# Masked queries copied inside SBUF, transfers planned as one line of work, last set divided through a shuffle

## The chip, the cores and the metric

One core of a Trainium2 chip runs the whole kernel. The metric is the time of one execution on the device in microseconds (us); the median of the runs counts. The engines are PE (matrix multiply), ACT (activation functions), DVE (vector), POOL (GpSimd) and SP, which here only issues transfers.

## What is computed

```python
xn = _layernorm(A_x)                      # x: 1 x 2048 x 512, bf16
q, k, v = split(xn @ wqkv)                # 32 heads of 16
p = softmax(q @ k.T * 16 ** -0.5)         # per head, 2048 x 2048
A = (p @ v) @ wo
y = _layernorm(xn)
B = gelu(y @ w1 + b1) @ w2 + b2           # w1: 512 x 1792
out = A_x + A + B
```

There are 32 x 2048 x 2048 scores, 134 million, and each needs an exponential.

## The kernel before

**Tiling.** The queries come in four tiles of 512 columns. A *set* `g` is four heads of one query tile, so there are 32 sets, and a *unit* is one head of a set against 128 keys: a matmul of 32 rows (16 of a head, 16 of its neighbour) that gives 128x512 scores in one PSUM bank (`qk`, line 1163). There are 2048 units. A stored query tile holds two heads in 32 rows; for each of them a *masked* copy is needed in which the rows of the other one are zero, and this is `qz`.

**Two ways to an exponential.** Most units go to ACT, two or three banks in one instruction (line 1383). The rest go in fours to DVE, which approximates the exponential with integer arithmetic: one pass per unit (line 1480) and three passes over all four (line 1501), so that PE has four terms to add up where ACT leaves one (`pv`, line 1181). Which unit goes which way is settled while the program is built.

**The plan.** All instructions are put into the order of each engine by a planner, `_Plan`, that simulates the engines with durations written into the calls of `add`. `lat` is the time from the end of an instruction to its effect, above all from a transfer's issue to its landing. The table `PICK` overrides single choices: at step n it names the operation to take. Engines run strictly in the order so made, and so does the queue of SP: a transfer whose wait isn't over holds back all behind it.

**Masked queries** (`build_q`, lines 1018 to 1043). DVE scales the projected queries into `qc` (line 1031). A transfer writes `qc` into `zdram`, in DRAM, between rows that two transfers have set to zero at the start; two more read it back into `qz` at two row offsets, and so get the zeros along. They wait for the first to land. This happens 15 times.

**The other transfers on SP.** `ydram<-ys` writes the normalized rows for the MLP, 16 times; `ys` has two buffers, so DVE's next row (line 896) waits for the write of the last but one. For each pair of sets `build_opost` sends the sums to DRAM (`ldram`, line 1536), moves half the heads between partitions (`osb<-osb`, four transfers of 16x512, line 1540), reads the sums back in another shape (`lc`, line 1550), takes reciprocals (line 1554) and spreads them (`rdram`, `rlb`). The weights `w_r`, the bias and the outputs also go through SP.

**The last set** (`build_opost_last`) does without DRAM. In two halves of 256 columns DVE transposes 32x32 blocks out of PSUM (line 1598), takes the reciprocal of 8 columns of sums (1603), multiplies (1604) and transposes back (1607). POOL checks the sums (1613, 1615), and the result of all checks becomes a flag that decides whether a slow general version must run.

Of the kernel before, what the change touches and what calls it, by code (L numbers as in the profile page):

```python
# [50 lines left out]
class _Op:  # L51
# [3 lines left out]
                 "at", "feeds")  # L55
# [5 lines left out]
class _Plan:  # L61
# [28 lines left out]
    def add(self, eng, dur, fn, deps=(), prio=0.0, acq=(), rel=(), lat=0.0, dense=0.0, nb=0.0,  # L90
            mode=None, spare=False, feeds=False, hold=0):
        op = _Op()
        op.spare, op.feeds = spare, feeds
# [40 lines left out]
    def run(self):  # L134
# [8 lines left out]
        while self.left:  # L143
# [56 lines left out]
            op.end, op.at = end, t  # L200
            free[op.eng] = end
# [16 lines left out]

    pe_log = ()
# [266 lines left out]
def kernel(  # L486
# [47 lines left out]
    zdram = drp.tile([2, 2 * P, QW], BF, name="zdram")  # L534
# [88 lines left out]
    def act(cols):  # L623
# [1027 lines left out]
    def build_mlp(qt):  # L1651
# [44 lines left out]
        for x, (fc, n, pr) in enumerate(last):  # L1696
# [17 lines left out]
            if f1 > f0:  # L1714
                g = add("ACT", act((f1 - f0) * QW), lambda f0=f0, f1=f1: soft(1, f0, f1), [g], hi + 5)
# [203 lines left out]
```

## Time and profile before

| | us |
|---|---|
| median of 3 runs | 763.32 |
| lowest and highest run | 760.44, 763.65 |
| profiled execution | 769.47 |
| its span | 767.6 |
| PE busy in it | 736.1 (96%) |
| ACT busy | 736.0 (96%) |
| DVE busy | 701.0 (91%) |
| POOL busy | 47.4 (6%) |
| mean granted clock of PE | 0.989 |

The span runs from the first to the last instruction of the profiled execution; 1.9 us of its time lie outside. A part of what PE does is filler (lines 1318, 1857 and 1862, multiplications by zero), which the planner puts where PE would stand idle. So the busy share of PE says little, and the busy shares of ACT and DVE have to be read stretch by stretch.

### The profile page before, as it was taken

To read this page: it belongs to the slowest core of one execution; us is meant where nothing else is said; L and a number is where in the kernel's file an instruction comes from. 1 tells how busy PE (TensorE), PEld (TensorE's weight loads), DVE (VectorE), ACT (ScalarE), POOL (GpSimd) and SP (SyncE) were. 2 spreads that over 40 slices of the span, in tenths; PEclk is the share of its full clock that TensorE was granted. 3 is DMA by queue.
4 is the path that set the end of the run, shared out by engine and by line. 5 is a ranking of instruction groups with operands and counts; after the bars stand their busy time and mean duration, and the time that the engine had idled before them with its cause. 6 is when DMAs were issued, how large, how long until landed. Compare 5 with 4: busy or idle time off the path is not lost.

```text
span 767.6 us, 23191 instructions
## 1 busy us (share of the span) xinstructions
PE 736.1 (96%) x9941; PEld 246.1 (32%) x9943; DVE 701.0 (91%) x1187; ACT 736.0 (96%) x663; POOL 47.4 (6%) x78
## 2 busy tenths in 40 slices
PE   8999999999999999999998999999999999999997
PEld 4433333333332332233332233333322233333332
DVE  7968999999999998999888999989999999898895
ACT  6996999999999999999998999999999999999996
POOL 3500000000010010000002000000001000100010
PEclk9998999999999999999998999999999999999999
DMA  7233312102122341101055010102125202221001
GB/s 217 68 84 118 73 24 59 43 20 50 36 65 44 81 102 32 49 9 38 16 112 140 22 50 19 32 29 60 48 58 123 46 26 56 57 59 37 25 3 44
DMA packets 72858, 43.58 MB, mean 57 GB/s; under 512 B 49140, under 2 KB 65524, under 8 KB 72752
## 3 DMA queue, kind: packets, MB, share of 16 engines
q1 hardware_dynamic: 69456, 37.35, 18.4%
q0 software_dynamic: 2336, 4.20, 2.7%
q8 instruction: 78, 1.28, 0.7%
q10 hardware_dynamic: 960, 0.52, 0.3%
q14 instruction: 28, 0.23, 0.1%
HBM read 28.18 MB, written 7.19 MB: 46 GB/s over the span
## 4 chain that ended last, share of the span: by engine, by line
ACT 35%; PE 34%; DVE 13%; issue 12%; DMA 3%; SPq 1%; POOL 0%; DVEq 0%; ACTq 0%; POOLq 0%
ACT p_sb L1383 31%; PE ps L1181 12%; PE ps L1163 11%; PE ps L607 10%; DVE x_sb L1480 5%; DVE it L1501 4%; ACT ht L1688 2%; DMA lc<-ldram 1%; DVE it L1480 1%; ACT ht L1707 1%; DMA ydram<-ys 1%; PE ps L1862 1%; SPq L1540 1%; DMA ldram<-osb 1%; DVE osb L1534 1%
## 5 line engine op out<-in xcount | busy, mean ns | idle before, releaser
L1383 ACT ACTIVATE p_sb<-ps 128x1536 bf16<-128x1536 f32 (+1 forms) x619 | 695.8, 1272 | 16.6 <-PE ps L1163 15.1
L1163 PE MATMUL ps<-qz,kt 32*128 32x512 bf16 x2048 | 310.6, 385 | 18.7 <-ACT p_sb L1383 10.2
L1480 DVE TENSOR_SCALAR x_sb<-ps 128x512 int16<-128x512 f32 x420 | 279.0, 686 | 18.2 <-PE ps L1163 17.1
L1501 DVE TENSOR_SCALAR it<-x_sb 128x2048 int16<-128x2048 int16 x315 | 211.6, 690 | 3.1 <-PE ps L1181 2.0
L1163 PEld LDWEIGHTS <-kt 32*128 32x128 bf16 x2048 | 83.8, 91 | 271.5 <-issue 265.1
L1181 PE MATMUL ps<-p_sb,va 128*32 128x512 bf16 x1520 | 149.6, 392 | 0.8 <-DVE va L1063 0.4
L1181 PE MATMUL ps<-it,va 128*32 128x512 f16 x1692 | 137.7, 383 | 0.7 <-DVE it L1501 0.5
L1181 PEld LDWEIGHTS <-va 128*32 128x32 bf16 x3632 | 75.8, 95 | 135.7 <-issue 109.8
L1318 PE MATMUL ps<-ones_bf,zeros_bf 32*128 32x512 bf16 x280 | 101.5, 386 | 0.0
L1480 DVE TENSOR_SCALAR it<-ps 128x512 int16<-128x512 f32 x108 | 72.3, 686 | 5.2 <-PE ps L1163 4.8
L607 PE MATMUL ps<-yT,w_r 128*32 128x512 bf16 x896 | 59.2, 386 | 2.3 <-DVE x_sb L1480 1.8
L607 PE MATMUL ps<-w_sb,ht 128*32 128x512 bf16 x896 | 59.5, 381 | 0.0
L1501 DVE TENSOR_SCALAR it<-it 128x2048 int16<-128x2048 int16 x81 | 54.7, 688 | 0.8 <-PE ps L1181 0.4
L1729 POOL DMA_DIRECT2D wkv<-in_A_x_dram x16 | 16.7, 1056 | 448.1 <-DMA wkv<-b_f 325.3
L1181 PE MATMUL ps<-x_sb,va 128*32 128x512 f16 x420 | 41.9, 386 | 0.0
L1676 DVE TENSOR_SCALAR ht<-ps,b_sb 128x512 bf16<-128x512 f32 x40 | 29.9, 746 | 1.8 <-PE ps L607 1.7
L607 PEld LDWEIGHTS <-w_r 128*32 128x32 bf16 x896 | 21.0, 96 | 28.7 <-issue 14.3
L1862 PE MATMUL ps<-ones_bf,zeros_bf 128*32 128x512 bf16 x312 | 28.3, 386 | 0.0
L1318 PEld LDWEIGHTS <-zeros_bf 32*128 32x128 bf16 x280 | 24.7, 91 | 10.5 <-issue 9.8
L607 PEld LDWEIGHTS <-ht 128*32 128x32 bf16 x896 | 20.3, 96 | 23.5 <-issue 9.8
L1534 DVE COPY osb<-ps 128x512 f32<-128x512 f32 x31 | 21.3, 686 | 2.4 <-PE ps L1181 1.8
L607 PE MATMUL ps<-wkv,xnT 128*32 128x128 bf16 x1024 | 18.0, 225 | 0.9 <-DVE va L1063 0.8
(97 smaller groups left out, 296.6 us busy)
## 6 DMA issues: line engine op xcount, KB each, us to landing
w_r<-in_B_w_dram SPq DMA_DIRECT2D x56, 128.0 KB
rlb<-rdram SPq DMA_DIRECT2D x16, 256.0 KB
wkv<-b_f SPq DMA_DIRECT2D x16, 256.0 KB
wkv<-in_A_x_dram POOLq DMA_DIRECT2D x16, 256.0 KB, 3.9
qz<-zdram SPq DMA_DIRECT2D x30, 128.0 KB
ydram<-ys SPq DMA_DIRECT2D x16, 128.0 KB
zdram<-qc SPq DMA_DIRECT2D x15, 128.0 KB
osb<-osb SPq DMA_DIRECT2D x60, 32.0 KB
```

What stands on the lines that cost most here:

```text
L607: I(nc.tensor.matmul(dst[32 * j:32 * j + 32], lhsT=lhsT[:, 32 * j:32 * j + 32], rhs=rhs, start=start, stop=stop, tile_position=(0, 32 * j)))
L1163: I(nc.tensor.matmul(ps[:, bank, :], lhsT=kt[lo:lo + 32, s // 2, k * P:(k + 1) * P], rhs=qz[lo:lo + 32, (qt * NB + s // 2) % NQB, s % 2, : ...
L1181: I(nc.tensor.matmul(ps[32 * j:32 * j + 32, o_bank[g], :], lhsT=vals[:, h * VS:h * VS + 32], rhs=wts(j), start=pv_done[g] == 1, stop=end, ...
L1318: I(nc.tensor.matmul(ps[:, o_bank[g], :], lhsT=zeros_bf[32 * j:32 * j + 32, :], rhs=ones_bf[32 * j:32 * j + 32, :], start=False, stop=Fals ...
L1383: exp_inst.append(I(nc.scalar.activation(p_sb[:, s0:s1, :].rearrange("p a b -> p (a b)"), ps[:, b0:b0 + n, :].rearrange("p a b -> p (a b)" ...
L1480: I(nc.vector.tensor_scalar(out=ib[sl][:, j, :], in0=ps[:, pool.bank(key), :], scalar1=LEVEL, scalar2=0.0, op0=ALU.add, op1=ALU.max))
L1501: I(nc.vector.tensor_scalar(out=tb[x].rearrange("p j q -> p (j q)"), in0=ib[sl].rearrange("p j q -> p (j q)"), scalar1=float(SHIFT[t]), sc ...
L1534: e0 = add("DVE", dve(QW), lambda: I(nc.vector.tensor_copy(osb[:, e, :], ps[:, o_bank[g], :])), pv_ops[g] + list(osb_use.get(e, ())), pr - ...
L1676: I(nc.vector.tensor_scalar(out=hq[:, fc, :], in0=ps[:, misc.bank(key), :], scalar1=b1_sb[:, fc:fc + 1], scalar2=None, op0=ALU.add))
L1688: I(nc.scalar.activation(out=hv, in_=hv, func=AF.Gelu_apprx_tanh, scale=1.0))
L1729: return add("POOL", 1.0, lambda: I(nc.gpsimd.dma_start(out=acc[:, c, :], in_=x2[qi * P:(qi + 1) * P, :], accum_op=ALU.add)), (xb_,), pr - ...
L1862: I(nc.tensor.matmul(ps[32 * j:32 * j + 32, bank, :], lhsT=zeros_bf[:, 0:32], rhs=ones_bf[:], start=new, stop=new, tile_position=(0, 32 * ...
```

## The change

**Masked queries.** `zdram` and its transfers are gone. POOL sets three of the four `qz` buffers to zero once, and each time eight transfers of 16x512 copy the rows of a head from `qc` straight into `qz`, inside SBUF. Only these rows are ever written, so the zeros stay.

**Transfers in the planner.** Most transfers no longer have a fixed `lat`. They have `work`, the time that they occupy the DMA rings, and the planner lets them queue: one starts 0.5 us after its issue or when those ahead are through, and has landed 0.65 us after its work. ACT's gelu is planned 0.09 us longer.

**The last set.** For each half a shuffle copies the row of sums to the 32 rows of its group, DVE takes the reciprocal of all 256 columns and multiplies straight out of PSUM. The check is done behind both halves by DVE: one transpose of all 512 columns and two comparisons.

**Smaller things.** The accumulating transfers of `x` are planned one behind the other, POOL has a `drain` behind the last, and the identity matmuls at the end no longer wait in the plan for the last exponential but for the last scores. `PICK` is a new table, so the order is new on all engines; the constants that say which sets are meant for DVE are the same. The exponentials on ACT become 280 of three units and 336 of two.

```diff
+            if op.work is not None:
+                self.rings = max(end + self.DMA0, self.rings) + op.work
+                op.lat = self.rings + self.DMA1 - end
...
+    DMA0, DMA1 = 0.5, 0.65
+    rings = 0.0
...
-    zdram = drp.tile([2, 2 * P, QW], BF, name="zdram")
...
     PICK = {
-        29: 30, 69: 45, 83: 62, 86: 63, 99: 54, 104: 57, 107: 49, 128: 75, 130: 72, 133: 69, 141: 73,
+        64: 334, 65: 43, 127: 75, 158: 80, 169: 192, 170: 81, 173: 79, 185: 113, 191: 90, 197: 88,
...
             yw_op[t] = dma("SP", ydram[t * P:(t + 1) * P, :], ys[:, t % 2, :], (y_op[t],), prio=pr,
-                           lat=2.5)
+                           work=0.3)
...
+    mk_z = [None] + [add("POOL", 0.95, lambda n=n: I(nc.gpsimd.memset(qz[:, n], 0.0)), (), 10.0 + n, nb=12.0)
+                     for n in range(1, NQB)]
...
-        zd = zdram[n % 2]
-        w = dma("SP", zd.rearrange("(b z r) q -> b z r q", z=2, r=DH)[:, 0],
-                qc[:, n % 2, :], [e, mk_z[n % 2]] + qz_rd.get(n - 2, []), prio=pr - 600, lat=2.4)
...
         for par in range(2):
-            src = bass.AP(zd.tensor, zd.offset + par * DH * QW, [[4 * DH * QW, HS], [QW, 2 * DH], [1, QW]])
-            o = dma("SP", qz[:, n % NQB, par, :], src, [w] + old, prio=pr - 599 + par, lat=4.6)
+            for j in range(HS):
+                rows = slice(32 * j + DH * par, 32 * j + DH * par + DH)
+                o = dma("SP", qz[rows, n % NQB, par, :], qc[rows, n % 2, :],
+                        [e, mk_z[n] if n < NQB else None] + old, prio=pr - 600 + par, work=0.1)
+                qc_use[n].append(o)
...
         l_op[e] = add("SP", 0.5, lambda: I(nc.sync.dma_start(dram, osb[DH:P:32, e, :])), [e0], pr - 500,
-                      lat=L1)
+                      work=0.05)
...
-                 [l_op[0], l_op[e]], pr - 500, lat=L2)
+                 [l_op[0], l_op[e]], pr - 500, work=0.1)
...
-            e0 = add("DVE", 0.36, lambda qs=qs: I(nc.vector.transpose(
-                out=ta[:, qs], in_=ps[:, o_bank[g], qs])), pv_ops[g] + h_use[0] + [e1], pr,
-                rel=(o_done(g),) if hf else ())
...
+            def f0(qs=qs):
+                I(nc.vector.stream_shuffle(ta[:, qs], ps[:, o_bank[g], qs], [DH] * 32))
+            e0 = add("DVE", 0.4, f0, pv_ops[g] + h_use[0] + [e1], pr)
+
+            def f1(qs=qs):
+                I(nc.vector.reciprocal(out=ta[:, qs], in_=ta[:, qs]))
+                I(nc.vector.tensor_tensor(out=ons[:, slot, qs], in0=ps[:, o_bank[g], qs], in1=ta[:, qs],
                                           op=ALU.mult))
-                I(nc.vector.transpose(out=ons[:, slot, qs],
-                                      in_=on_t[:, cs].rearrange("p c r -> p (c r)")))
...
+        def f2():
+            I(nc.vector.transpose(out=tl[:], in_=ps[:, o_bank[g], :]))
+            for k, (lim, op) in enumerate(((L_MIN, ALU.is_ge), (L_MAX, ALU.is_le))):
+                I(nc.vector.tensor_scalar(out=okl[:, k, :], in0=tlv[:, :, DH], scalar1=lim,
+                                          scalar2=None, op0=op))
```

**What stands where.** SP in the first 60 us, around the first masked queries; before, from the transposes of the keys' rows on:

```order
L852 DMA_TRANSPOSE xnT<-yT 128x4x128 x3
L730 DMA ydram<-ys 128x512 x2
L852 DMA_TRANSPOSE xnT<-yT 128x4x128
L730 DMA zdram<-qc 8x16x512
L730 DMA ydram<-ys 128x512 x2
L730 DMA qz<-zdram 128x1x512 x2
L730 DMA ydram<-ys 128x512 x4
L906 DMA w_sb<-in_B_w_dram 128x14x512
```

and now, from the writes of `ys` ahead of these transposes on:

```order
L741 DMA ydram<-ys 128x512 x9
L864 DMA_TRANSPOSE xnT<-yT 128x4x128 x4
L741 DMA qz<-qc 16x512 x8
L741 DMA ydram<-ys 128x512 x7
L918 DMA w_sb<-in_B_w_dram 128x14x512
```

The two reads that wait for the write to DRAM no longer stand between the writes of `ys`; eight copies stand ahead of the last seven of these.

DVE at the same place, from the scaling of these queries (`qc`) on, before:

```order
L1031 TENSOR_SCALAR qc<-ps 128x512
L896 TENSOR_SCALAR ys<-x_sb,mv,r_105 128x512 x2
L1009 CAST kt<-ps 128x512
L896 TENSOR_SCALAR ys<-x_sb,mv,r_105 128x512
L1009 CAST kt<-ps 128x512
L896 TENSOR_SCALAR ys<-x_sb,mv,r_105 128x512
L1063 CAST va<-ps 128x4x8x16
L1480 TENSOR_SCALAR x_sb<-ps 128x512
L896 TENSOR_SCALAR ys<-x_sb,mv,r_105 128x512
```

and now:

```order
L1041 TENSOR_SCALAR qc<-ps 128x512
L908 TENSOR_SCALAR ys<-x_sb,mv,r_104 128x512
L1488 TENSOR_SCALAR x_sb<-ps 128x512
L908 TENSOR_SCALAR ys<-x_sb,mv,r_104 128x512
L1488 TENSOR_SCALAR x_sb<-ps 128x512
L1509 TENSOR_SCALAR it<-x_sb 128x2048 x3
L1021 CAST kt<-ps 128x512
L1071 CAST va<-ps 128x4x8x16
L1488 TENSOR_SCALAR x_sb<-ps 128x512
L908 TENSOR_SCALAR ys<-x_sb,mv,r_104 128x512
L1488 TENSOR_SCALAR x_sb<-ps 128x512
L908 TENSOR_SCALAR ys<-x_sb,mv,r_104 128x512
```

The rows `ys` stood close behind one another, and now the passes of the DVE exponentials (`x_sb`, `it`) and the copies `kt` and `va` lie between them.

DVE at the end of the program, from the division of the last set on, before:

```order
L1598 STREAM_TRANSPOSE ht<-ps 128x256
L1603 RECIPROCAL rl_t<-ht 128x8
L1604 TENSOR_TENSOR ht<-ht,rl_t 128x256
L1607 STREAM_TRANSPOSE ons<-ht 128x256
L1598 STREAM_TRANSPOSE ht<-ps 128x256
L1603 RECIPROCAL rl_t<-ht 128x8
L1604 TENSOR_TENSOR ht<-ht,rl_t 128x256
L1607 STREAM_TRANSPOSE ons<-ht 128x256
L1807 TENSOR_TENSOR yT<-ps,wkv 128x512
L1630 TENSOR_REDUCE flag_i<-ps 1x1
```

and now:

```order
L1605 STREAM_SHUFFLE ht<-ps 128x256
L1609 RECIPROCAL ht<-ht 128x256
L1610 TENSOR_TENSOR ons<-ps,ht 128x256
L1605 STREAM_SHUFFLE ht<-ps 128x256
L1609 RECIPROCAL ht<-ht 128x256
L1610 TENSOR_TENSOR ons<-ps,ht 128x256
L1617 STREAM_TRANSPOSE ht<-ps 128x512
L1619 TENSOR_SCALAR okl<-ht 128x16 x2
L1818 TENSOR_TENSOR yT<-ps,wkv 128x512
L1634 TENSOR_REDUCE flag_i<-ps 1x1
```

The reciprocal is taken of 256 columns where it was of 8, the second transpose of each half is gone, and the check stands ahead of the last output row (`yT`).

## Rows read from the trace of the kernel before

**Rows 1.** Busy time in three stretches (columns first, x counts instructions)

```profile
core 0: us, PE busy (x) PEld busy (x) DVE busy (x) ACT busy (x) POOL busy (x), PEclk, DMA share, GB/s
0.00:20.00 20.00, 16.85 (x174) 7.86 (x177) 14.86 (x41) 12.53 (x19) 7.32 (x21) 1.00 0.70 211
20.00:755.00 735.00, 711.41 (x9690) 235.39 (x9689) 679.93 (x1134) 718.45 (x640) 38.62 (x54) 0.99 0.21 53
755.00:767.60 12.60, 7.84 (x80) 2.83 (x77) 6.24 (x14) 5.06 (x6) 1.44 (x4) 1.00 0.14 45
```

**Rows 2.** Groups by line: busy us, mean ns, idle before; exponentials also by form

```profile
L1383 ACT ACTIVATE p_sb<-ps 128x1536 bf16<-128x1536 f32 (+1 forms) x619 | 695.8, 1272 | 16.6 <-PE ps L1163 15.1 <-ACT p_sb L1383 0.2
L1383 ACT ACTIVATE p_sb<-ps 128x1536 bf16<-128x1536 f32 x282 | 423.9, 1503 | 6.3 <-PE ps L1163 5.6
L1383 ACT ACTIVATE p_sb<-ps 128x1024 bf16<-128x1024 f32 x337 | 356.5, 1078 | 10.2 <-PE ps L1163 9.5 <-ACT p_sb L1383 0.2
L1480 DVE TENSOR_SCALAR x_sb<-ps 128x512 int16<-128x512 f32 x420 | 279.0, 686 | 18.2 <-PE ps L1163 17.1 <-PE ps L1318 0.3
L1501 DVE TENSOR_SCALAR it<-x_sb 128x2048 int16<-128x2048 int16 x315 | 211.6, 690 | 3.1 <-PE ps L1181 2.0
```

**Rows 3.** ACT's waits in 50:66, 396:416, 574:600 (us in total, times, longest)

```profile
ACT p_sb L1383 <- PE ps L1163: 5.6, 3, 3.3
ACT p_sb L1383 <- PE ps L1163: 3.8, 4, 1.5
ACT p_sb L1383 <- PE ps L1163: 1.1, 2, 0.9
```

**Rows 4.** Timeline, 50 to 57 us: SP and DVE (start, duration, idle before)

```profile
50.46 1.16 SPq L730 DMA_DIRECT2D qz<-zdram  x2
51.29 0.41 DVE L896 TENSOR_SCALAR ys<-x_sb,mv,r 128x512 bf16<-128x512 bf16 x1 [3.02 <-DMA ydram<-ys]
56.74 0.41 DVE L896 TENSOR_SCALAR ys<-x_sb,mv,r 128x512 bf16<-128x512 bf16 x1 [2.20 <-DMA ydram<-ys]
```

**Rows 5.** Busy time beside the first wait, behind the second; PEclk third from end

```profile
48.00:52.00 4.00, 4.00 (x72) 1.44 (x74) 0.98 (x3) 3.73 (x5) 0.00 (x0) 1.00 0.37 104
58.00:64.00 6.00, 5.49 (x95) 2.67 (x98) 3.86 (x7) 1.94 (x2) 0.00 (x0) 0.50 0.13 44
```

**Rows 6.** Timeline: two reciprocals of the sums that waited for their transfer

```profile
403.83 0.35 DVE L1554 RECIPROCAL rc<-lc 128x32 f32<-128x32 f32 x1 [1.92 <-DMA lc<-ldram]
582.37 0.35 DVE L1554 RECIPROCAL rc<-lc 128x32 f32<-128x32 f32 x1 [1.13 <-DMA lc<-ldram]
```

**Rows 7.** Chain of work that ended last: start, us from issue to landing

```profile
47.91 3.25 DMA ydram<-ys
400.86 2.95 DMA lc<-ldram
577.56 4.79 DMA lc<-ldram
```

**Rows 8.** Issue times on SP: min/median/max ns

```profile
L1540 SPq DMA_DIRECT2D osb<-osb x60: 528/582/1609, 77.8 to 719.1; - x60
L730 SPq DMA_DIRECT2D qz<-zdram x30: 518/557/957, 50.5 to 681.1; - x30
```

**Rows 9.** Timeline of the last 10 us: the last set is divided

```profile
758.97 0.45 DVE L1598 STREAM_TRANSPOSE ht<-ps 128x256 f32<-128x256 f32 x1 [1.57 <-PE ps L1181]
761.66 0.45 DVE L1607 STREAM_TRANSPOSE ons<-ht 128x256 bf16<-128x256 bf16 x1
762.61 0.69 DVE L1807 TENSOR_TENSOR yT<-ps,wkv 128x512 bf16<-128x512 f32 x1 [0.51 <-PE ps L607]
```

**Rows 10.** Reciprocals by form (busy us, mean ns of one, idle before)

```profile
L1554 DVE RECIPROCAL rc<-lc 128x32 f32<-128x32 f32 x15 | 5.2, 349 | 4.3 <-DMA lc<-ldram 4.3
L1603 DVE RECIPROCAL rl_t<-ht 128x8 f32<-128x8 f32 x2 | 0.4, 204 | 0.1
L1554 DVE RECIPROCAL rc<-lc 128x16 f32<-128x16 f32 x1 | 0.2, 246 | 0.0
```

More of the change, by code (lines that the diff above doesn't have):

```diff
@@ L54 @@
                  "done", "dense", "mode", "seq", "spare",
-                 "at", "feeds")
+                 "at", "feeds", "work")
     def __init__(self):
@@ L90, in add @@
     def add(self, eng, dur, fn, deps=(), prio=0.0, acq=(), rel=(), lat=0.0, dense=0.0, nb=0.0,
-            mode=None, spare=False, feeds=False, hold=0):
+            mode=None, spare=False, feeds=False, hold=0, work=None):
         op = _Op()
+        op.work = work
         op.spare, op.feeds = spare, feeds
@@ L618, in mmd, with gel @@
         return n * (cols / 2400.0 + 0.005)
+    def gel(cols):
+        return act(cols) + 0.09
     def dve(cols, rate=1.042):
@@ L726, in held, with dma @@
             tc.add_manual_dep(inst.ins, exp_inst[-2].ins.name, SYNC_DEP, reason="its turn")
-    def dma(eng, dst, src, deps=(), prio=0.0, lat=2.0, nb=0.0):
+    def dma(eng, dst, src, deps=(), prio=0.0, lat=2.0, nb=0.0, work=None):
         def fn():
@@ L732, in fn @@
                 held(d)
-        return add(eng, 0.5, fn, deps, prio, lat=lat, nb=nb)
+        return add(eng, 0.5, fn, deps, prio, lat=lat, nb=nb, work=work)
     ld_x = {}
@@ L916 @@
     ld_wo = [dma("SP", wo_r[:], A_wo.rearrange("(b p) c -> p b c", p=P), (ld_w2,), prio=110.0, nb=110.0,
-                 lat=6.0)]
+                 work=2.5)]
     wo_v = A_wo.rearrange("(b j e r) c -> b j e r c", b=NB, j=HS, e=2, r=DH)
@@ L1014 @@
     qc_use = {}
-    qz_rd = {}
-    mk_z0 = add("POOL", 0.9, lambda: I(nc.gpsimd.memset(ons[:], 0.0)), (), 0.0)
-    mk_z = [dma("SP", zdram[n].rearrange("(e p) q -> p e q", e=2), ons[:], (mk_z0,), prio=10.0, lat=3.0,
-                nb=16.0) for n in range(2)]
+    mk_z = [None] + [add("POOL", 0.95, lambda n=n: I(nc.gpsimd.memset(qz[:, n], 0.0)), (), 10.0 + n, nb=12.0)
+                     for n in range(1, NQB)]
     def build_q(qt, b):
@@ L1541, in build_opost @@
                 osb[32 * j + DH:32 * j + 32, 0, :], osb[32 * j:32 * j + DH, 1, :])),
-                [e0, l_op[0]], pr - 400, lat=LM) for j in range(HS)]
+                [e0, l_op[0]], pr - 400, work=0.2) for j in range(HS)]
             osb_use[1] = moved + [l_op[1]]
@@ L1557, in build_opost @@
             back[:].rearrange(flat, f=w) if single else back.rearrange(flat, f=w), rcv)), [e2], pr - 500,
-            lat=L1)
+            work=0.1)
         e3 = add("SP", 0.5, lambda: I(nc.sync.dma_start(
             rlb[:], bcast(back[:] if single else back, 32 if single else DH))), [e3] + last_rlb, pr - 500,
-            lat=L3 if single else 4.5)
+            work=3.0 if single else 1.9)
         e4 = add("DVE", dve(QW), lambda: I(nc.vector.tensor_tensor(
@@ L1617, in build_opost_last @@
-            e2 = add("POOL", 0.5, f2, [e0, e2], pr)
+        tlv = tl.rearrange("p (c r) -> p c r", r=32)
+        def f2():
[3 more added lines that the diff above has]
+                                          scalar2=None, op0=op))
+        e2 = add("DVE", 0.9, f2, [e1, e2], pr - 5, rel=(o_done(g),))
@@ L1647, in w1_load @@
         return dma("SP", w1_r[:, n % NW1], w1_view[:, :, fc * P:(fc + 1) * P],
-                   list(w1_use[n - NW1] if n >= NW1 else ()) + [st_op[NT - 1]], pr - 12, lat=WLAT,
+                   list(w1_use[n - NW1] if n >= NW1 else ()) + [st_op[NT - 1]], pr - 12, work=0.7,
                    nb=pr - 18)
@@ L1656, in build_mlp @@
             out=yT[:], in_=ydram[qt * QW:(qt + 1) * QW, :])),
-            y_use + [yw_op[4 * qt + i] for i in range(4)] + list(xn_op.values()), lo - 8, lat=YLAT,
+            y_use + [yw_op[4 * qt + i] for i in range(4)] + list(xn_op.values()), lo - 8, work=1.6,
             nb=lo - 12)
@@ L1690, in fg @@
         def fg():
-            gelu_end[0] = I.now + act((2 * FC - ND) * QW) + ND * act(QW) + 2.0
+            gelu_end[0] = I.now + act((2 * FC - ND) * QW) + ND * gel(QW) + 2.0
             phase["left"] = phase["act"] = ND
@@ L1714, in build_mlp @@
             if f1 > f0:
-                g = add("ACT", act((f1 - f0) * QW), lambda f0=f0, f1=f1: soft(1, f0, f1), [g], hi + 5)
-            g = add("ACT", act(QW) + (1.5 if fc == FC - 1 else 0.0), fd, (m, g), hi + 5,
+                g = add("ACT", gel((f1 - f0) * QW), lambda f0=f0, f1=f1: soft(1, f0, f1), [g], hi + 5)
+            g = add("ACT", gel(QW) + (1.5 if fc == FC - 1 else 0.0), fd, (m, g), hi + 5,
                     rel=(idle.giver(key),))
@@ L1722 @@
     ot_use, acc_op = {}, {}
+    last_x = []
     def sums(qi, pr):
@@ L1727, in sums, with last @@
         wait = [acc_op.get(c)] + list(kt_op.values()) + list(va_op.values())
-        xb_ = dma("SP", acc[:, c, :], b2_all, wait + [mk_b2], pr - 30, lat=3.5, nb=pr - 45)
-        return add("POOL", 1.0, lambda: I(nc.gpsimd.dma_start(
-            out=acc[:, c, :], in_=x2[qi * P:(qi + 1) * P, :], accum_op=ALU.add)), (xb_,), pr - 20, lat=XL)
+        xb_ = dma("SP", acc[:, c, :], b2_all, wait + [mk_b2] + last_x, pr - 30, nb=pr - 45, work=1.6)
+        def last():
+            I(nc.gpsimd.dma_start(
+                out=acc[:, c, :], in_=x2[qi * P:(qi + 1) * P, :], accum_op=ALU.add))
+            if qi == NT - 1:
+                I(nc.gpsimd.drain())
+        last_x[:] = [add("POOL", 1.0, last, (xb_,), pr - 20, work=0.8)]
+        return last_x[0]
     def heads(qt, bs, cs):
```

40 lines of the change are left out of this document (13 added, 27 removed), and 58 rows, old and new, of the table PICK.

## The prediction

> **What bounds the kernel now.** I read the busy times of three stretches first [rows 1]. ACT is busy for 736.04 of the 767.6 us, and its idle time lies in three places: 20 − 12.53 = 7.5 us at the start, 12.6 − 5.06 = 7.5 us at the end, and 735 − 718.45 = 16.55 us in the middle. So in the middle ACT works for 98% of the time, and the kernel can become shorter in three ways only: less work on ACT, fewer waits of ACT in the middle, or a shorter end. DVE is idle for 735 − 679.9 = 55 us of the middle, PE fills its gaps with multiplications by zero, and neither is the bound.
>
> Then the waits of ACT by stretch [rows 3]. Of the 16.55 us, 5.6 lie at 50 to 66 us, 3.8 at 396 to 416 and 1.1 at 574 to 600, together 10.5; always it is PE's scores that come late. The timeline shows what lies behind the first [rows 4]: DVE stood for 3.02 and again for 2.20 us before a row of `ys`, until the write of an earlier row to `ydram` had landed. SP had issued the two reads of `zdram` (50.46 to 51.62 us) between these writes. One such write needed 3.25 us from issue to landing [rows 7]. While DVE stands, PSUM banks aren't emptied and PE runs out of work; the granted clock then fell to half, from 2.4 to 1.2 GHz, and stayed there from 58 to 64 us, in which ACT worked for 1.94 of 6 us [rows 5]. So the price of a late transfer isn't its own length but what PE loses after it. The other two places begin alike: DVE's reciprocal stood for 1.92 and 1.13 us until the sums (`lc`) had come back [rows 6], after 2.95 and 4.79 us of transfer [rows 7].
>
> **The change, part by part.** *Work on ACT.* There were 282 exponentials of three units and 337 of two [rows 2], 1520 units; now there are 280 and 336, 1512. The group is busy for 695.8 us, 0.458 a unit, so eight units fewer are −3.7 us. They lie on ACT's path throughout, and the whole of it counts. DVE gets them as two groups of four, with eight passes of 0.686 and six of 0.690 us [rows 2], 9.6 us. Its 55 idle us hide that; without this cover it would cost up to 9.6.
>
> *The end.* The division of the last set lies on the path: nothing else is left to do. It now takes from 758.97 to 762.11 us, 3.1 us [rows 9]. In the new form each half has a shuffle and a multiplication out of PSUM; the nearest row is the transpose of 256 columns, 0.45 us, and I take that for both. Between them stands a reciprocal of 256 columns, which the trace does not have. It has 8, 16 and 32 columns in 204, 246 and 349 ns [rows 10]: 5.3 and then 6.4 ns for each further column. With 6.0 to 6.4 the 256 columns take 1.70 to 1.78 us, and I take 1.75. The upper bound, were the slope to rise by the same step again to 7.6 ns, is 2.05; the lower is what the other passes of 256 columns need, 0.45. Both halves then take 2 x (0.9 + 1.75) = 5.3 us, +2.2 (bounds −0.4 and +2.8). Behind them DVE now does the check, a transpose of 512 columns (0.69 as for `yT` [rows 9]) and two comparisons (about 0.2 each by the shortest reciprocal [rows 10]), 1.1 us, ahead of the last output row. That row already waited 0.5 us for PE [rows 9], so +0.6. Together the end costs +2.8 us, between +0.2 and +3.4. What POOL did for the check lay beside other work, and its end saves nothing.
>
> On the reciprocal the Trainium skill says, in "VectorE: DVE Perf Modes", section "First, the fixed hardware budget", that it is an iterative divide with a repeat count of 8. By its clock of 0.96 GHz that makes 8.3 ns a column and an estimate of 2.1 us for 256; the sum would be 0.7 us higher. The rows agree that it costs several times a plain pass, and show 6 ns, not 8.
>
> *The waits.* At 50 to 66 us the reads that waited are gone from SP's queue. In their place stand eight copies of 16x512. The like of them, `osb<-osb`, takes 582 ns to issue [rows 8], so the eight hold SP for some 5.0 us, and the next write of `ys` is issued 5 us after `qc` is done. In DVE's new order `ys`, `x_sb`, three `it`, `kt`, `va` and `x_sb` stand before the first row that needs its buffer back, some 5.5 us. With a write of 3.25 us [rows 7], or of half of that, DVE still waits, for 1 to 2.7 us, but once instead of twice; the first wait of 3.02 us alone had cost ACT 0.27 us (3.73 of 4 busy from 48 to 52 [rows 5]), it was the second that emptied PE. I put 1.0 us in place of 5.6. At 396 to 416 and 574 to 600 us the planner now lets the return of the sums queue behind the weights, and no read of `zdram` stands ahead of `lc`. I put 1.5 for 3.8 and 0.6 for 1.1. That is −4.6 − 2.3 − 0.5 = −7.4 us. It could be nothing, if the copies delay as much as the reads did, or −10.5 if all three go.
>
> *Without effect on the sum.* Three settings to zero on POOL in place of one: POOL is busy for 7.3 of the first 20 us [rows 1], and nobody waits for these until the first copy. The two transfers that cleared `zdram`, and the identity matmuls that may run earlier: PE has nothing else to do beside the division. The longer plan for gelu and the `drain` move no work onto ACT; if the drain held up POOL's last check by a microsecond it would still be done before the last set is divided.
>
> *The sum*, against the profiled execution: 769.5 − 3.7 + 2.8 − 7.4 = 761.2 us. The median of the runs is 6.15 us below that execution. ACT's work is the same in all of them, so I read the difference as fewer waits, 16.55 − 6.15 = 10.4 us in the middle, and scale the gain by 10.4/16.55 to −4.7: 763.3 − 3.7 + 2.8 − 4.7 = **757.8 us**.
>
> **The rivals.** *The reciprocal costs like any pass.* Then the end costs +0.2 and not +2.8: 755.2 us. For it speaks only that the three rows are short ones; their slope speaks against it.
>
> *The copies hold up SP.* SP's part in one set of masked queries grows from about 0.6 + 2 x 0.56 = 1.7 us (the reads by [rows 8], the write taken like a copy) to 5.0 us, 15 times. What stands behind comes 3.3 us later, and the writes of `ys` and the reciprocals wait as before: the gain of 4.7 is lost, 762.5 us, no change. For it speaks the estimate above that DVE still waits; against it, that all reads that wait for a landing are gone. In the Trainium skill, "DMA: Bandwidth & Descriptors", section "Rules for kernel authors", many small transfers should be joined into a large one, since under 64 KB one pays mostly overhead. By that rule eight copies of 16 KB are worse than the three of 128 KB; the rows bear it out for the issue, not for the landing.
>
> *The plan expects the sums too early.* This one ends slower. Where nothing queues, the planner now has `lc` landed 1.25 us after its issue is over, where it had 3.2. The trace shows 2.95 and 4.79 us from the start of the issue [rows 7], 2.4 and more from its end. So DVE reaches its reciprocal earlier and stands there at each of the 15 pairs of sets, where now 4.3 us in all are lost to it [rows 10]. At 582 us a wait of 1.13 went with 1.1 us of idle ACT [rows 3, 6]. If all 15 cost that, it is +16.5 us: 774 us. From nine of them on the kernel is slower than before by half a per cent. Against it: the two rows are the late ones, and the other pairs kept within the plan.
>
> **How the numbers follow.** A difference under 0.5%, 3.8 us, can hardly be told from none. I give the forecast (around 757.8, its own range 753 to 761) a chance of 0.50, the cheap reciprocal 0.12, the copies on SP 0.25, the late sums 0.13. Faster means below 759.5: most of the first, all of the second, little of the third, 0.58. Slower means above 767.1: nearly all of the last, 0.13. The rest, 0.29, is no change. The range goes down to 752, where the end costs +0.2 and all three waits go (10.5, scaled to 6.6: 763.3 − 3.7 + 0.2 − 6.6 = 753.2) and a little of the remaining waits too, and up to 767, where the third case also has the dearest end and a wait more.
>
> **What would show it.** In the profile of the changed kernel: 616 exponentials with about 692 us; two reciprocals of 256 columns near 1.75 us, and 5.3 us from the first shuffle to the second product; no stretch at half the clock around 58 us, at most one wait of `ys` for `ydram`; issues of the copies near 0.6 us; ACT idle for about 9 us between 20 us and the last exponentials. The forecast is wrong if the clock falls to half in two or more stretches, if DVE's reciprocals of the sums wait for more than some 8 us in all, or if the last division takes under 3 or over 6.5 us.

## Result and profile after

| | before | after |
|---|---|---|
| median | 763.23 us (6 runs) | 768.45 us (6 runs) |
| lowest and highest run | 760.36, 763.65 | 767.37, 769.00 |
| profiled execution | 769.47 | 769.00 |
| its span | 767.6 | 767.2 |
| mean granted clock of PE | 0.989 | 0.995 |

The ratio is 1.0077, interval 1.0057 to 1.0097: the changed kernel is **slower by 0.8%**. Forecast were 757.8 us and a range that ended at 767. The two profiled executions are equal within half a microsecond. So what was added there is about as long as what was removed; that ordinary runs lack most of the removed part, the first experiment shows.

The stretches of the profile, as in [rows 1] (PE, PEld, DVE, ACT, POOL busy, then clock, DMA share, GB/s):

```profile
0.00:20.00 20.00, 15.30 (x182) 6.87 (x182) 15.35 (x39) 12.50 (x19) 9.01 (x21) 1.00 0.63 184
20.00:753.00 733.00, 711.00 (x9796) 238.04 (x9797) 690.82 (x1152) 719.37 (x639) 37.64 (x56) 1.00 0.19 48
753.00:767.20 14.20, 5.70 (x52) 2.05 (x44) 7.08 (x13) 1.69 (x4) 0.00 (x0) 0.71 0.12 40
```

ACT idles for 733 − 719.4 = 13.6 us of the middle, where it idled for 16.55; 9 were forecast. The last set's division begins 5.3 us earlier than before (753.69 instead of 758.97 us), and yet the span ends only 0.4 us earlier.

The group of the exponentials on the page, as in [rows 2] (busy us, mean ns, idle before):

```profile
L1391 ACT ACTIVATE p_sb<-ps 128x1536 bf16<-128x1536 f32 (+1 forms) x616 | 693.5, 1268 | 13.6 <-PE ps L1171 10.6
```

616 of them are busy for 693.5 us, where the forecast had about 692. The waits of ACT and DVE between 20 and 753 us, as in [rows 3, 4, 6] (us in total, times, longest):

```profile
ACT p_sb L1391 <- PE ps L1171: 10.2, 29, 1.8
...
DVE rc L1562 <- DMA lc<-ldram: 5.0, 7, 1.0
DVE ys L908 <- DMA ydram<-ys: 1.7, 1, 1.7
```

ACT waits for scores 29 times, 10.2 us in all; before it was 24 times and 15.1 us, 10.5 of them at the three places of [rows 3]. Now only one wait is longer than 1 us. The busy time in the two stretches that [rows 5] and [rows 6] belong to:

```profile
56.00:64.00 8.00, 7.63 (x155) 3.02 (x147) 7.41 (x14) 7.70 (x9) 0.00 (x0) 1.00 0.20 55
396.00:416.00 20.00, 18.28 (x236) 6.06 (x229) 18.87 (x33) 19.24 (x18) 6.36 (x8) 1.00 0.58 136
```

The clock is 1.00 in both, and ACT works for 7.70 of 8 and 19.24 of 20 us. The issue times of the copies, as in [rows 8] (min/median/max in ns, first and last start):

```profile
L741 SPq DMA_DIRECT2D qz<-qc x120: 507/587/1938, 43.7 to 684.9; - x120
```

A copy takes 0.587 us to issue, as estimated. The timeline of the end, as in [rows 9, 10] (start, duration, idle before):

```profile
753.69 0.45 DVE L1605 STREAM_SHUFFLE ht<-ps 128x256 f32<-128x256 f32 x1
754.17 1.75 DVE L1609 RECIPROCAL ht<-ht 128x256 f32<-128x256 f32 x1
...
758.58 0.42 DVE L1610 TENSOR_TENSOR ons<-ps,ht 128x256 bf16<-128x256 f32 x1
...
759.06 1.04 PE L611 MATMUL ps<-wo_l,ons 128*32 128x512 bf16 x8 [1.35 <-DVE ons L1610]
...
761.09 0.31 DVE L1634 TENSOR_REDUCE flag_i<-ps 1x1 int32<-1x160 f32 x1 [0.17 <-PE ps L1629]
```

The reciprocal takes 1.75 us and both halves 5.3, as forecast. The flag of before, from the same timeline:

```profile
763.22 0.30 DVE L1630 TENSOR_REDUCE flag_i<-ps 1x1 int32<-1x160 f32 x1
```

The clock of the changed kernel between the second product and the flag (third number from the end):

```profile
758.80:761.30 2.50, 2.00 (x16) 0.80 (x16) 1.99 (x6) 0.58 (x1) 0.00 (x0) 0.55 0.18 61
```

PE stood for 1.35 us until the last product was there; its clock is at 1.2 GHz for nearly all of this stretch, and the last eight matmuls need 1.04 us. From the first shuffle to the end of the flag it is 7.7 us, and from there 5.8 us to the end of the span: before 4.55 and 4.06.

### The profile page after: what moved, and what is told of

It reads as the page before. It is cut to its first block, busy times and chain, and to the rows that moved or that the text cites. A ratio compares the mean times of both kernels' runs of the same rounds, so it can differ in the third digit from the quotient of the medians.

```text
span 767.2 us, 23441 instructions
## 1 busy us (share of the span) xinstructions
PE 732.0 (95%) x10017; PEld 247.0 (32%) x10017; DVE 713.2 (93%) x1204; ACT 733.6 (96%) x660; POOL 46.7 (6%) x76
## 3 DMA queue, kind: packets, MB, share of 16 engines
q1 hardware_dynamic: 66752, 32.90, 16.6%
## 5 line engine op out<-in xcount | busy, mean ns | idle before, releaser
L1391 ACT ACTIVATE p_sb<-ps 128x1536 bf16<-128x1536 f32 (+1 forms) x616 | 693.5, 1268 | 13.6 <-PE ps L1171 10.6
L1509 DVE TENSOR_SCALAR it<-x_sb 128x2048 int16<-128x2048 int16 x318 | 214.0, 691 | 1.5
L1189 PE MATMUL ps<-it,va 128*32 128x512 f16 x1720 | 140.3, 381 | 0.6 <-DVE it L1509 0.5
L1326 PE MATMUL ps<-ones_bf,zeros_bf 32*128 32x512 bf16 x291 | 104.8, 382 | 0.0
L1488 DVE TENSOR_SCALAR it<-ps 128x512 int16<-128x512 f32 x112 | 75.5, 687 | 5.7 <-PE ps L1171 5.2
L1509 DVE TENSOR_SCALAR it<-it 128x2048 int16<-128x2048 int16 x84 | 57.0, 689 | 0.4
L1873 PE MATMUL ps<-ones_bf,zeros_bf 128*32 128x512 bf16 x352 | 30.5, 385 | 0.0
L611 PEld LDWEIGHTS <-w_r 128*32 128x32 bf16 x896 | 21.2, 96 | 25.2 <-issue 10.2
L1692 ACT ACTIVATE ht<-ht 128x3584 bf16<-128x3584 bf16 (+1 forms) x8 | 18.5, 2342 | 0.0
```

The lines of the kernel that those rows point to most:

```text
L611: I(nc.tensor.matmul(dst[32 * j:32 * j + 32], lhsT=lhsT[:, 32 * j:32 * j + 32], rhs=rhs, start=start, stop=stop, tile_position=(0, 32 * j)))
L1189: I(nc.tensor.matmul(ps[32 * j:32 * j + 32, o_bank[g], :], lhsT=vals[:, h * VS:h * VS + 32], rhs=wts(j), start=pv_done[g] == 1, stop=end, ...
L1326: I(nc.tensor.matmul(ps[:, o_bank[g], :], lhsT=zeros_bf[32 * j:32 * j + 32, :], rhs=ones_bf[32 * j:32 * j + 32, :], start=False, stop=Fals ...
L1391: exp_inst.append(I(nc.scalar.activation(p_sb[:, s0:s1, :].rearrange("p a b -> p (a b)"), ps[:, b0:b0 + n, :].rearrange("p a b -> p (a b)" ...
L1488: I(nc.vector.tensor_scalar(out=ib[sl][:, j, :], in0=ps[:, pool.bank(key), :], scalar1=LEVEL, scalar2=0.0, op0=ALU.add, op1=ALU.max))
L1509: I(nc.vector.tensor_scalar(out=tb[x].rearrange("p j q -> p (j q)"), in0=ib[sl].rearrange("p j q -> p (j q)"), scalar1=float(SHIFT[t]), sc ...
```

## The experiments

Kernels named b_ are the kernel before with an edit, those named a_ the changed one. All compute the whole result. The runs of the kernel before beside each group had medians of 762.0 to 762.2 us.

**Which time is the kernel's own?** *b_again* is the kernel before without any edit.

> The kernel before, not changed in anything, run again with its own profile, since the forecast took the waits of one profiled execution (769.5 us) as a sample of the runs that make the median (763.2 us). Theory A (the waits that the change takes away are rare): an execution of about 763 us shows none of the two half-clock stretches at 50 to 66 us and 396 to 416 us; from 20 us to the last exponential ScalarE idles about 10 us, not 16.5, and the mean granted clock is 0.995 or more. Theory B (they are in every run, and the profiled one is longer for something else): an execution of 763 us shows both stretches, and ScalarE idles 15 us or more; the 6 us then lie at the start or at the end.

Measured: 762.55 us (12 runs from 759.83 to 765.99), ratio 1.0006 (0.9985 to 1.0027). The profiled execution took 759.83 us with a clock of 0.999. Its busy times in the middle and in the stretch of [rows 5], and the waits from 50 to 66 us (us in total, times, longest):

```profile
20.00:749.00 729.00, 707.04 (x9725) 235.35 (x9724) 679.81 (x1133) 720.12 (x640) 36.54 (x52) 1.00 0.21 53
...
58.00:64.00 6.00, 5.70 (x180) 3.03 (x173) 5.51 (x10) 5.68 (x7) 0.00 (x0) 1.00 0.49 153
...
DVE ys L896 <- DMA ydram<-ys: 4.5, 2, 3.3
ACT p_sb L1383 <- PE ps L1163: 1.8, 3, 1.3
```

ACT idles for 729 − 720.1 = 8.9 us of the middle, and from 58 to 64 us it works for 5.68 of 6 us, where [rows 5] had 1.94. Theory A holds for this execution, which was the fastest of the twelve; none of the median length was profiled. DVE waits for its buffer here too, for 4.5 us in two waits where it was 5.2 [rows 4]. What is missing is what came behind: the clock stays at 1.00, and ACT loses 1.8 us in place of 5.6. At 396 to 416 and 574 to 600 us it loses 0.7 and 0.9, so 3.4 at the three places where [rows 3] had 10.5. In the profiles of *b_newdiv* and *b_pad64* (below), whose order ahead of the last set is that of before, ACT idles for 10.8 and 13.7 us from 20 us to the last exponential. The 24 runs of the kernel before in that group go from 759.5 us at a clock of 1.00 to 766.1 at 0.993. So the loss behind the waits differs from run to run, and the first profile had most of it.

**The parts alone.** *b_copies* has the copies, with the settings of `qz` to zero that they need, and nothing else of the change; the rows of PE, DVE and ACT are those of before.

```diff
-        w = dma("SP", zd...[:, 0], qc[:, n % 2, :], ...)
+        # nothing
         for par in range(2):
-            o = dma("SP", qz[:, n % NQB, par, :], src, [w] + old, ...)
+            for j in range(HS): nc.sync.dma_start(qz[rows, n % NQB, par, :], qc[rows, n % 2, :])
```

> The kernel before with the masked queries by eight copies inside SBUF alone: four copies stand where each of the two reads of zdram stood, nothing stands where the write stood, and the rows of TensorE, VectorE and ScalarE are word for word those of before. Theory A (ordinary runs hardly wait for the masked queries): 762 to 764 us, ratio 0.998 to 1.002. Theory B (the copies bring what the forecast gave them, the whole wait at 50 us with its half clock): 758 to 761 us. Rival C (sixteen halves of a microsecond more of issues hold up SyncE's queue): 765 to 767 us, with more waits of ScalarE around the sets' closings.

Measured: 775.68 us, ratio 1.0168 (1.0137 to 1.0198). None of the three expected 13.6 us. The timeline of SP's queue (start, duration from first to last issue):

```profile
48.25 5.65 SPq L1049 DMA_DIRECT2D qz<-qc  x8
53.99 5.54 SPq L730 DMA_DIRECT2D ydram<-ys  x4
```

The copies hold SP for 5.65 us, and the writes of `ys` are issued behind them. DVE and ACT in the same timeline:

```profile
57.84 0.41 DVE L896 TENSOR_SCALAR ys<-x_sb,mv,r 128x512 bf16<-128x512 bf16 x1 [3.33 <-DMA ydram<-ys]
...
62.37 1.94 ACT L1392 ACTIVATE p_sb<-ps 128x1024 bf16<-128x1024 f32 x2 [4.47 <-PE ps L1172]
```

DVE stands for 3.33 us until such a write has landed, and then ACT for 4.47. So rival C has the mechanism, at a far higher price. ACT idles for 4.0 us at 425 us too, and for 0.8 to 1.9 at 66, 89, 298, 302, 589, 594 and 700 us. Not all of the 13.6 us is the queue: in the profiled execution 1.5 us more lie behind the flag than in *b_again* (table below). Without an order made for them the copies are the dearest part of the change.

*b_newdiv* has the new division alone:

```diff
-            e0 = ... nc.vector.transpose(out=ta[:, qs], in_=ps[:, o_bank[g], qs])
+            e0 = ... nc.vector.stream_shuffle(ta[:, qs], ps[:, o_bank[g], qs], [DH] * 32)
-                reciprocal of 8 columns, tensor_tensor, transpose
+                reciprocal of ta[:, qs], tensor_tensor out of ps
```

> The kernel before with the last set's division by shuffle and reciprocal of 256 columns alone, check on VectorE; the order of everything ahead of the last set stays. Theory D (the loss is at the end): the last set's division and the flag take 3.2 us longer than before and the stretch behind the flag up to 1.7 us longer, so 766.5 to 768.5 us, ratio 1.004 to 1.007. Rival E (the end of the program is set by something else, and the loss of the changed kernel lies in its new order): 763 to 764.5 us.

Measured: 767.49 us, ratio 1.0075 (1.0048 to 1.0102). From the first step of the division to the flag 8.15 us instead of 4.55, from there to the end 6.08 instead of 4.06. Theory D holds for this kernel: the new division alone loses as much as the whole change, though 2.0 us of it lie behind the flag, where PE's branch is late (below).

*a_olddiv* puts the old division into the changed kernel (the same edit backwards).

> The changed kernel with the old division of the last set (transpose, reciprocal of 8 columns, product, transpose; check on GpSimd) put back; all else, the new order too, stays. Theory D (the loss is at the end): 3.2 us less for the division and the flag, and up to 1.7 us less behind the flag: 763.5 to 765.3 us, even with the kernel before within 0.3%. Rival E (the loss lies in the new order ahead of the last set): 767 to 768.5 us. Theory of the forecast, with the division taken out of its sum: 755 us.

Measured: 765.07 us, ratio 1.0048 (1.0026 to 1.0069), by the ratios 2.2 us less than the changed kernel, though the two intervals overlap. The division and flag take 4.84 us again. But from the flag to the end it is 6.71 us, more than with the new division: something at the end belongs to neither form. And 3.7 us of loss remain, so D isn't the whole.

**What remains.** *a_latezero* lets the three settings to zero wait for the first exponential:

```diff
-    mk_z = ... add("POOL", 0.95, lambda n=n: I(nc.gpsimd.memset(qz[:, n], 0.0)), ...)
+    # behind exp_inst[0], n = 1 to 3:
+    z = I(nc.gpsimd.memset(qz[:, n], 0.0)); add_manual_dep(z, exp_inst[0], SYNC_DEP)
```

> The changed kernel with the three settings of qz to zero (GpSimd) moved behind the first exponential by a wait; the rest of the order stays. Theory F (at 7.4 to 10.5 us they slow VectorE's two normalisations, 2.05 us for both instead of 0.73, and so everything behind them): both take 0.4 us each again, the first exponential starts at 11.6 instead of 12.6 us, and the time falls by 1.0 us. Rival G (VectorE waited for something else there): the two rows stay at 1 us each or the first exponential stays at 12.5, and the time stays.

Measured: 766.32 us, ratio 1.0054 (1.0034 to 1.0075). The timeline of POOL and DVE in the changed kernel (start, duration):

```profile
7.43 3.02 POOL L1027 MEMSET qz<- 128x1024 bf16 x3
...
7.51 2.05 DVE L857 TENSOR_SCALAR yT<-x_sb,mv,r 128x512 bf16<-128x512 bf16 x2 [0.26 <-POOL r L840]
```

And of DVE with the later settings:

```profile
7.38 0.73 DVE L857 TENSOR_SCALAR yT<-x_sb,mv,r 128x512 bf16<-128x512 bf16 x2 [0.27 <-POOL r L840]
```

Theory F holds in its mechanism: the two normalizations take 0.73 instead of 2.05 us, and the first exponential starts at 11.19 instead of 12.63. What it brings in time is less sure: the intervals of 1.0054 and of the changed kernel's 1.0077 overlap, and the first exponential varies for other reasons too (table below; in *a_best*, with the later settings, it starts at 12.85). On the cause the Trainium skill states in "SBUF — State Buffer", section "Who interferes with whom", that GpSimd's ports are VectorE's second pair, and that when VectorE runs in a mode that needs this pair, as a tensor_scalar can, whoever issues first holds it for the whole instruction and the other one stands. The trace agrees: the two passes lasted 1.01 and 1.11 us, about as long as one filling each (0.94 to 1.09 us); which port they waited for, no run shows.

*a_nodrain* leaves out `nc.gpsimd.drain()`.

> The changed kernel without the drain on GpSimd. Forecast's view (the drain costs nothing): time of the changed kernel within 0.15%. Rival H (the drain holds up the end): the 5.8 us from the flag to the end of the span shrink to the 4.1 us of before and the time falls by 1.7 us. If they stay at 5 to 7 us, SyncE's stop of some 2 us behind its branch, seen in the changed kernel and not in the one before, has another cause.

Measured: 768.43 us, ratio 1.0090 (1.0062 to 1.0118); 6.27 us from the flag to the end. The time is within 0.15% of the changed kernel's 1.0077, as the forecast's view has it; the intervals allow a difference of 0.3%. The end is late without the drain too.

*a_dram* sends the masked queries through `zdram` again, in the new order: a write in place of the first copy, two reads in place of the last two.

> The changed kernel with its masked queries through zdram again (one write and two reads where the first and the last two of the eight copies stood); order on TensorE, VectorE and ScalarE as in the changed kernel. Theory J (the new order itself has more small waits of ScalarE, 13.5 us from 20 us to the last exponential where the kernel before has 8.6): the time stays within 1.5 us of the changed kernel, and 12 us or more of waits remain. Theory K (the eight copies hold up SyncE in the new order too): 3 us or more are gained and the waits fall below 10 us. If the route through memory is worse in this order: 770 us or more.

Measured: 772.61 us, ratio 1.0137 (1.0117 to 1.0157); ACT waits for scores for 18.3 us in 37 times. The last answer on record holds: in this order the copies are worth 4.6 us by the ratios, the opposite sign of *b_copies*, and more than that at an equal end, since *a_dram* ends early (3.6 us behind the flag, where the changed kernel has 5.8). K falls. J holds in that waits remain without the copies, but its time was wrong: 32 gaps of ACT of 0.15 to 0.6 us, together 9.8, are there without them. That the copies have no part in the gaps of the changed kernel isn't shown, since the route through DRAM brings waits of its own.

*b_ys4* gives the kernel before four buffers for `ys`:

```diff
-                    out=ys[:, t % 2, :], ...
+                    out=(ot if t & 2 else ys)[:, t % 2, :], ...
```

> The kernel before with four buffers for the rows ys on their way to ydram instead of two (the other two lie in ot, which is not in use yet); order unchanged. Theory L (the stretches at 50 to 90 us of the kernel before come from VectorE's waits for a buffer of ys, and runs differ in how long these are): no wait of ys for ydram is left, 758 to 760.5 us with a narrower spread. Rival M (they come from the masked queries): 762 us and the same spread.

Measured: 761.07 us (759.75 to 764.0), ratio 0.9976 (0.9955 to 0.9997). No wait of `ys` is left and the wait at 58 us is gone, as theory L has it; one of 2.8 us at 400 us, behind the sums, is still there. The time falls less than theory L had it (758 to 760.5 us).

**The last instructions.** The trace's records list the branches. Behind the flag each engine loads it and branches over the general version. The table has the stations of the profiled executions in us (the first exponential starts at different times in kernels that are alike up to there: from 11.30 to 13.27 in the rows b_ but *b_copies*; in *a_pad64* PE had a mean clock of 0.83 in the first 20 us); the last columns are the time from SP's branch to its next instruction and the number of SP's instructions ahead of the branch.

| kernel | first exp. | last exp. ends | division starts | flag ends | span ends | SP's step | SP's instr. |
|---|---|---|---|---|---|---|---|
| before | 12.96 | 758.40 | 758.97 | 763.52 | 767.6 | 0.76 | 523 |
| b_again | 11.59 | 748.87 | 749.43 | 753.98 | 758.0 | 0.79 | 523 |
| b_copies | 12.94 | 764.46 | 765.02 | 769.57 | 775.1 | 1.88 | 592 |
| b_newdiv | 11.31 | 750.45 | 751.05 | 759.20 | 765.3 | 0.55 | 523 |
| b_ys4 | 11.30 | 750.05 | 750.61 | 755.16 | 759.2 | 0.74 | 523 |
| after | 12.63 | 753.03 | 753.69 | 761.40 | 767.2 | 2.40 | 591 |
| a_again | 13.03 | 752.03 | 752.69 | 760.30 | 766.3 | 2.61 | 591 |
| a_olddiv | 12.46 | 751.67 | 752.30 | 757.13 | 763.8 | 3.30 | 591 |
| a_latezero | 11.19 | 753.12 | 753.77 | 760.82 | 766.9 | 2.77 | 591 |
| a_nodrain | 14.10 | 752.97 | 753.62 | 760.67 | 766.9 | 2.92 | 591 |
| a_dram | 11.79 | 760.57 | 761.60 | 769.30 | 772.9 | 0.55 | 515 |
| a_pad24 | 12.54 | 750.27 | 750.93 | 757.97 | 761.6 | 0.53 | 615 |
| a_pad64 | 16.07 | 754.49 | 755.15 | 762.86 | 766.5 | 0.53 | 655 |
| b_pad64 | 13.27 | 755.39 | 755.95 | 760.50 | 764.6 | 0.75 | 587 |
| a_lzpad | 11.03 | 749.90 | 750.55 | 757.60 | 761.2 | 0.53 | 615 |
| a_divpad | 12.46 | 750.53 | 751.15 | 755.99 | 759.6 | 0.53 | 615 |
| a_best | 12.85 | 750.55 | 751.18 | 756.01 | 759.6 | 0.54 | 655 |

In *b_newdiv* it is PE, with eight instructions more than before, that needs 4.2 us at its branch, and SP 0.55. *a_pad64* and *a_pad24* put idle instructions into SP's program, and *b_pad64* into that of before:

```diff
+            if qi == 5:      # behind this output row
+                for _ in range(64): I(nc.sync.drain())
```

> The changed kernel with 64 instructions that do nothing (drains of SyncE) in SyncE's program behind one output row at about 400 us, where it is idle; no transfer and no order changes. So far SyncE's first instruction behind its branch at the end came 0.6 to 0.8 us after the branch in the kernels with 515 to 523 instructions ahead of it and 1.9 to 3.3 us in those with 591 or 592 (the ones with eight copies). Theory N (where the branch stands in SyncE's program decides whether its target has to be fetched first): with 655 instructions the step takes 0.8 us or less and the time falls by 2 us, to 766. Rival O (what the copies leave in the queues makes it late): 2 to 3 us remain, and the time stays.

> The same with 24 instead of 64 such instructions (615 ahead of the branch). Theory N leaves two answers open, by where the borders of the fetched pieces lie: either 2 to 3 us as in the changed kernel, or 0.8 us or less; a value between would speak against it. Rival O: 2 to 3 us.

> The kernel before with the same 64 instructions (587 ahead of the branch, near the 591 of the changed kernel). Theory N: the step behind SyncE's branch grows from 0.75 to 2 us or more, and the time by 1.3 us or more, to 763.5 us. Rival O: 0.75 us, time of the kernel before within 0.2%.

Measured: *a_pad64* 764.46 us (1.0026, 1.0007 to 1.0044) and *a_pad24* 764.68 us (1.0033, 1.0015 to 1.0050), with steps of 0.53 us; *b_pad64* 764.48 us (1.0021, 0.9995 to 1.0047), step 0.75. Rival O falls: the same copies with 24 more idle instructions leave no delay. But 587 instructions didn't bring it into the kernel before, against N's expectation; its times show no sure change. In the table the step is late in all six executions with 591 or 592 instructions ahead of the branch and in none of the eleven others (515 to 587, 615 and 655). That fits the place in the program, with borders that these runs don't locate; since only kernels with the copies have 591 or 592, it isn't shown that the number alone does it. That the target has to be fetched is argued, not shown. The two pads brought 3.4 us on average where the step and what hangs on it show 2.2 to 2.7 (5.8 to 6.3 us from flag to end with the new division, and 3.6 with a pad); the rest lies within the noise of the ratios.

**Do the terms add up?** On one more chip:

> The changed kernel, not changed in anything, on the chip of this comparison. On the first chip it had 768.4 us against 763.2, a ratio of 1.0077. If the terms of the forecast's miss are properties of the kernel and not of a chip: 767 to 768.5 us, ratio 1.006 to 1.009, SyncE's step behind its branch 2 to 3 us again, first exponential near 12.6 us.

> The changed kernel with the old division and 24 idle instructions of SyncE (its step behind the branch falls to 0.5 us). If the division costs its 2.9 to 3.2 us of the end in full: 764.6 of the kernel with the idle instructions alone less 3, 761 to 762 us. If a shorter division lays bare another late thing: 763 us or more.

> The changed kernel with the settings of qz to zero behind the first exponential and 24 idle instructions of SyncE; the new division stays. If the zeros cost 1.4 us at the start: 763 us. If the 2 us that their move brought came from elsewhere: 764.5 us, as with the idle instructions alone.

Measured: *a_again* 767.89 us, ratio 1.0073 (1.0050 to 1.0096), SP's step 2.61 us: the loss is the kernel's. *a_lzpad* (zeros later, 24 idle instructions) 763.67 us, 1.0019 (1.0006 to 1.0032). *a_divpad* (old division, 24 idle instructions) 762.85 us, 0.9999 (0.9978 to 1.0019). Taking 1% as 7.62 us:

| taken away | ratio from, to | us |
|---|---|---|
| SP's late branch | 1.0075, 1.0030 | 3.4 |
| new division, branch mended | 1.0033, 0.9999 | 2.6 |
| zeros beside DVE, branch mended | 1.0033, 1.0019 | 1.1 |

Each ratio is known to 0.1 or 0.2%, so each term to some 2 us; the term of the zeros isn't clear of nothing. Together they are 7.1 us, where 5.7 were lost, so they suffice for the loss. The 1.4 us that would be left to the new order and the copies are below what these ratios can tell.

**A version that beats both.** *a_best* is the changed kernel with the old division, the late zeros, four buffers of `ys`, no drain and 64 idle instructions.

> The changed kernel with what the runs so far found taken back or mended: the old division of the last set, the settings of qz to zero behind the first exponential, four buffers for ys, no drain, and 64 idle instructions of SyncE. If the terms add up (768.4 less 3.4 for the division, 2.0 for the zeros, 2.3 for the branch, 0.5 to 1 for the wait of ys): 760 us, a little faster than the kernel before. If the new order's small waits (13.5 instead of 8.6 us) are what counts and the terms overlap: 762 to 764 us.

Measured: 759.37 us (758.33 to 761.52), ratio 0.9950 (0.9929 to 0.9972). Busy time in its middle:

```profile
20.00:750.00 730.00, 710.12 (x9784) 237.28 (x9786) 691.46 (x1153) 718.59 (x639) 38.74 (x56) 1.00 0.19 48
```

ACT still idles for 11.4 us of the middle. The four buffers of `ys` are no part of the change, and they alone bring the kernel before to 0.9976 (*b_ys4*). The 2.0 us between the two ratios is what is left for the change itself, and their intervals overlap.

## Why the prediction was wrong

**What held.** The causes of the long waits were read rightly: no stretch at half the clock around 58 us, one wait of `ys` (1.7 us, in the forecast's 1 to 2.7), and DVE's reciprocals wait for 5.0 us in all, under the 8 that would have been a sign of being wrong. *b_ys4* shows that at 58 us it is the buffer of `ys`. The reciprocal and the division had their forecast 1.75 and 5.3 us. A copy takes the forecast time to issue, but the first eight held SP longer than the 5.0 us of the forecast: 5.65 us in *b_copies*, and 6.4 in `after`.

**The step that failed most: the gain by fewer waits,** −7.4 us in the profiled execution, scaled to −4.7 for the median. At the three places it came true against that execution: ACT waits for 2.0, 0.6 and 0.4 us there now, 3.0 in all, where 1.0, 1.5 and 0.6 were put. The total fits by luck, the single entries don't. Two things were wrong. First, the text saw that ordinary runs have fewer waits (10.4 us; *b_again* has 8.9), but scaled the gain as if the waits were shorter everywhere alike. What *b_again* lacks is just the loss at these places: 3.4 us where the first profile had 10.5, and with 3.0 left, 0.4 can be won there. Second, the text took the waits elsewhere, 6 us, over from the old order. *b_again* has 5.5 there, and the new order 10.6 in `after`. In the middle as a whole that is 13.6 us in `after`, and 11.4 in *a_best*. In `after` 29 gaps of ACT lasted 0.15 to 0.6 us, together 8.3; in *b_again* 14, together 3.4. Ahead of more than half of the late scores PE had just run a block of sixteen or more matmuls of the projections or the MLP; ahead of the scores that weren't late such a block stands about one time in seven. So this term was +4.7 us against the undisturbed execution of *b_again*, not −7.4. Against longer runs of before it is less: the profiles of the old order idle for 8.7 to 16.6 us from 20 us to the last exponential, those of the new one without `zdram` for 11.4 to 15.0. That the new waits lie in PE's order is argued from the trace; *a_dram* shows only that small gaps are there without the copies too.

**"Without effect on the sum"** was wrong for the three settings to zero: nobody waited for their result, but DVE stood still beside them, for 1.3 us (2.05 instead of 0.73). By ratios this was worth 1.1 to 1.6 us, neither of them clear of noise.

**The end,** +2.8 us, was right as far as the flag and lacked what comes behind it. From the division to the flag it took 7.7 us in `after`, +3.2, and 7.04 in *a_pad24*, +2.5. The difference goes with PE's clock ahead of the flag, 1.00 in *a_pad24*:

```profile
756.00:758.50 2.50, 1.13 (x16) 0.48 (x16) 1.94 (x6) 0.59 (x1) 0.00 (x0) 1.00 0.26 87
```

Sixteen matmuls take 1.13 us here and 2.00 in `after`, at 0.55. With this new division the clock fell in four of the eight profiled executions of the changed kernel and its variants (`after`, *a_again*, *a_pad64*, *a_dram*) and stayed in the others, so these 0.7 us aren't in every run. SP's step behind the branch was in no term and no row: in `after` it is 1.75 us more than before to the end of the span, and 2.2 more than with a pad; taking it away was worth 3.4 us by ratio.

**ACT's work,** −3.7 us, came out at 695.8 − 693.5 = −2.3. So this term was sized 1.4 us too large. The durations fell by 5.3 us (420.5 + 354.6 after, 780.4 in [rows 2]), but consecutive exponentials overlap, so neither sum is the busy time; the overlap fell from 84.6 to 81.6 us. That more gaps leave less overlap is argued.

**The rivals.** "The copies hold up SP" is what happens in the old order (*b_copies*), which lost 13.6 us in all; in the new order the wait for it is 1.7 us. "The plan expects the sums too early" did not come: DVE waited for `lc` 7 times, 1.0 us at most. The cheap reciprocal fell by its row. The time above 767 came from causes that no rival had.

Against the undisturbed execution of *b_again* (span 758.0) the changed one (767.2) has lost, by the stations above: 1.0 us until the first exponential, 3.1 until the last, 0.1 until the division, 3.2 until the flag, 1.75 until the end; 9.2 in all. The first part is no larger than the scatter of that station. The medians of before lie 2.2 to 3.4 us above that execution; that this is the loss behind the long waits, which the change would win back, fits the clocks of the runs and isn't measured.

The forecast's sum missed by 10.7 us (768.45 instead of 757.8). A gain of 4.7 that didn't come, 1.4 on ACT, 3.4 for SP's step and 1.1 for the zeros make 10.6; the terms are known less well than they fit.

## What to carry to other kernels

Before counting on a wait's removal, see in several executions what the wait costs: here DVE waited alike in two profiles, and ACT lost 5.6 us behind it in one and 1.8 in the other. A step that nobody waits for can still hold up an engine beside it, and a transfer split into eight is paid by the queue that issues it, so its order must be made for it. After every rewrite compare the stretch from the last flag to the end of the program, in which no work is listed.

## What the runs showed of the hardware

- A reciprocal of 128x256 f32 in SBUF takes 1.754 us, a shuffle of 256 columns out of PSUM 0.448 us.
- Beside GpSimd's settings of 128x1024 bf16 to zero (0.94 to 1.09 us each), VectorE's pass of 128x512 bf16 in SBUF took 1.01 and 1.11 us instead of 0.41; a cast out of PSUM beside the last of them took 0.67 us, no more than elsewhere.
- From SyncE's branch at the end to its next instruction it took 0.53 to 0.79 us in some programs and 1.9 to 3.3 us in others; 24 idle instructions ahead of it were enough to change it (2.40 to 0.53 us). TensorE once needed 4.2 us there.
- An exponential that follows another at once begins before that one's end: seven of 128x1024, 1.08 us each, took 6.52 us in a row, 0.93 each.
